# Per-head sums of squares on ScalarE, quarter-array raw products, one ring of PSUM banks and a new order, in a linear-attention plus gated-linear-unit kernel

## The chip, the cores and the metric

The kernel runs on one core of one Trainium2 chip. The metric is the device time of one execution in microseconds (us); a figure for a kernel is the median of its runs. The engines are TensorE (PE in the profile, with its weight loads as PEld), VectorE (DVE), ScalarE (ACT), GpSimd (POOL) and SyncE (SP, which here only issues DMAs). Each engine works through its own instructions in the order of the program, and waits on semaphores where it needs another's result.

## What is computed

The reference has two parts. The first is attention without a softmax, for 8 batches and 8 heads of 576 tokens and 64 columns; the second is a gated linear unit whose gate is a causal convolution over five tokens:

```python
kv = np.einsum('bhsd,bhse->bhde', k, v)
out = np.einsum('bhsd,bhde->bhse', q, kv)
rms = np.sqrt(np.mean(out * out, axis=-1, keepdims=True) + 1e-06)
x = out / rms * g_norm                    # then (B,H,S,D) -> (B, S, H*D): 8 x 576 x 512
xp = np.concatenate([np.zeros((B, K - 1, D)), x], axis=1)
for k in range(5):
    gate_pre += conv_w[k][None, None, :] * xp[:, k:k + S, :]
gate = 1.0 / (1.0 + np.exp(-gate_pre))
result = gate * (x @ w_val) @ w_out
```

q, k, v and the result are float32; the two weight matrices, 512 x 512, and conv_w arrive as float64 and are narrowed on the chip.

## The kernel before

All work is cut into small steps, and the text `PLAN` lists 1151 of them by name and arguments. The kernel runs through that list once and issues each step's instructions, so the list is the order of the work on every engine and in every DMA queue: two steps on one engine run in the listed order, and steps on different engines run as soon as what they wait for is there. There is no scheduler at run time.

A batch b has 576 tokens, in five chunks: 0 to 3 of 128 tokens and chunk 4 of 64. The steps of a batch, with the engine that does the work:

- `load_half`, `load_q`, `load_q_rows`, `stage_weight`: DMAs in, nearly all on SP's queue, with a few of the first on ACT's and POOL's queues. `narrow_weight w j n`, n from 0 to 7: the eight operations that turn a quarter of a float64 matrix into float32; n = 1, 2, 3 are ACT's, the others DVE's.
- `turn_q_rows` and `sort_q` (batches 0 and 1, PE and ACT) or `turn_q` (batches 2 to 7, DVE) put q with its columns on the partitions.
- `kv_product b i` (PE): k^T v of half of the heads, 36 products of 64 x 64 on the four quarters of the array, written at the front of `raws`. Between the two halves of batch 0 stand two filler products (`keep_warm 2`). `kv_copy b` (ACT, two instructions) moves the results into `kv_bd`, where two heads make one 128 x 128 block with zeros off the diagonal.
- The raw product q (k^T v): for batches 0 and 1 `raw_product b c` multiplies each chunk by the block-diagonal 128 x 128 matrices; for batches 2 to 7 `raw_pair b c` does two chunks at once as 64 products of 64 x 64 on quarters, and `raw_product b 4` does the last chunk with the blocks.
- `square b c` (ACT, one instruction for the whole chunk) writes the squares to SBUF, beside a 65th column that holds the epsilon; `sums b c` (DVE) adds each head's 65 columns up; `powers b c` (POOL) raises the sums to the power -1/2; `normalise b c` multiplies the raw product by that root, on DVE for batch 0 and on ACT for batches 1 to 7, where each head is one instruction. Two chunks of batch 0 take their roots from Newton steps on DVE (`roots`).
- x gets its columns onto the partitions through PE and ACT (`turn_x`, `keep_x`) or through DVE and small SBUF-to-SBUF DMAs issued by POOL (`turn_blocks`, `move_blocks`). `halo` (POOL) copies the convolution's overlap.
- The gate: `gate_start` (ACT), four `gate_tap` (DVE), `gate_end` (ACT, the sigmoid), `gated` (DVE, times the values).
- The values x w_val: `val_product` with `keep_val` for batches 0 and 1; for batches 2 to 7 a scheme with seven instead of eight block products (`x_sums`, `val_fast`, `val_keep`). The last product with w_out in pairs of batches: `out_product` with `keep_out`, or seven block products again (`token_sums`, `fast_product`, `fast_keep`); `store` sends the rows out.

PSUM has eight banks. Two of them are `raws`, kept for k^T v and most raw products; the other six are handed out by `ps(kind, ...)`: one of kind "tp" and five of kind "mm". Near the end `raws` is closed and its two banks serve the last products (`ends`). `warm_up`, near the head of the list, runs one Sigmoid on a single column.

Of the kernel before, what the change touches and what calls it, by code (L numbers as in the profile page):

```python
# [15 lines left out]
P = 128  # L16
# [3 lines left out]
load_q_rows 0 1; stage_weight cw 0; load_q_rows 0 0; load_half v 0 0; load_half k 0 0; load_half v 0 1;  # L20
load_half k 0 1; warm_up; stage_weight wval 1; stage_weight wval 0; start_warm 36; turn_q_rows 0 0;
turn_q_rows 0 1; narrow_weight cw 0 0; turn_q_rows 0 2; narrow_weight cw 0 1; narrow_weight cw 0 2; sort_q 0 0;
turn_q_rows 0 3; sort_q 0 1; turn_q_rows 0 4; narrow_weight cw 0 3; kv_product 0 0; sort_q 0 2;
load_q_rows 1 0; narrow_weight cw 0 4; narrow_weight cw 0 5; load_half k 1 0; sort_q 0 3; narrow_weight cw 0 6;
load_half v 1 0; narrow_weight cw 0 7; sort_q 0 4; load_q_rows 1 1; load_half k 1 1; stage_weight wval 2;
keep_warm 2; kv_product 0 1; stage_weight wval 3; turn_cw; load_half v 1 1; kv_copy 0; keep_cw;
narrow_weight wval 1 0; raw_product 0 3; load_half v 2 0; raw_product 0 2; square 0 3; raw_product 0 4;
sums 0 3; stage_weight wout 0; square 0 2; raw_product 0 1; square 0 4; powers 0 3; sums 0 2;
narrow_weight wval 1 1; sums 0 4; raw_product 0 0; load_half v 2 1; square 0 1; narrow_weight wval 0 0;
narrow_weight wval 0 1; powers 0 2; square 0 0; normalise 0 3; sums 0 1; turn_x 0 3; sums 0 0; keep_x 0 3;  # L30
powers 0 4; normalise 0 2; narrow_weight wval 1 2; narrow_weight wval 1 3; turn_x 0 2; normalise 0 4;
turn_q_rows 1 0; roots 0; keep_x 0 2; narrow_weight wval 0 2; turn_x 0 4; sort_q 1 0; turn_q_rows 1 1;
keep_x 0 4; narrow_weight wval 0 3; normalise 0 1; turn_q_rows 1 2; halo 0; sort_q 1 1; normalise 0 0;
turn_x 0 1; narrow_weight wval 1 4; kv_product 1 0; narrow_weight wval 0 4; keep_x 0 1; sort_q 1 2;
narrow_weight wval 0 5; turn_x 0 0; narrow_weight wval 1 5; narrow_weight wval 0 6; turn_q_rows 1 3;
keep_x 0 0; narrow_weight wval 0 7; gate_start 0 0; turn_q_rows 1 4; narrow_weight wval 1 6; kv_product 1 1;
sort_q 1 3; load_q 2 0; narrow_weight wval 1 7; gate_start 0 1; narrow_weight wval 2 0; val_product 0 0 1;
gate_start 0 2; narrow_weight wval 3 0; sort_q 1 4; load_q 2 1; gate_tap 0 2 3; kv_copy 1; gate_tap 0 0 3;
narrow_weight wval 3 1; raw_product 1 3; narrow_weight wval 2 1; gate_tap 0 1 3; load_half k 2 0;
raw_product 1 2; keep_val 0 0 1; gate_tap 0 0 2; square 1 3; narrow_weight wval 3 2; val_product 0 1 1;  # L40
sums 1 3; square 1 2; gate_tap 0 1 2; powers 1 3; narrow_weight wval 2 2; load_half k 2 1; gate_tap 0 2 2;
narrow_weight wval 2 3; stage_weight wout 2; raw_product 1 1; sums 1 2; narrow_weight wval 3 3;
narrow_weight wval 2 4; raw_product 1 0; keep_val 0 1 1; powers 1 2; square 1 1; narrow_weight wval 2 5;
normalise 1 3; val_product 0 0 0; load_q 2 2; gate_tap 0 0 1; sums 1 1; turn_q 2 0; normalise 1 2; powers 1 1;
turn_x 1 3; narrow_weight wval 3 4; val_product 0 1 0; narrow_weight wval 2 6; keep_x 1 3; load_q 2 3;
narrow_weight wval 3 5; square 1 0; narrow_weight wval 2 7; normalise 1 1; turn_x 1 2; sums 1 0;
raw_product 1 4; gate_tap 0 2 1; stage_weight wout 1; powers 1 0; kv_product 2 0; narrow_weight wout 0 0;
square 1 4; sums 1 4; narrow_weight wout 0 1; narrow_weight wval 3 6; kv_product 2 1; keep_x 1 2; turn_q 2 1;
powers 1 4; normalise 1 0; gate_tap 0 2 0; turn_x 1 1; load_q 3 0; val_product 0 2 1; narrow_weight wval 3 7;
keep_x 1 1; gate_tap 0 1 1; keep_val 0 1 0; narrow_weight wout 0 2; gate_tap 0 1 0; keep_val 0 0 0; turn_x 1 0;  # L50
normalise 1 4; gate_tap 0 0 0; val_product 0 2 0; narrow_weight wout 2 0; narrow_weight wout 0 3; keep_x 1 0;
narrow_weight wout 0 4; kv_copy 2; val_product 0 3 1; turn_q 2 2; keep_val 0 2 1; keep_val 0 2 0; turn_q 2 3;
narrow_weight wout 2 1; load_q 3 1; gate_end 0 0; narrow_weight wout 0 5; turn_x 1 4; narrow_weight wout 0 6;
raw_pair 2 3; keep_val 0 3 1; keep_x 1 4; gated 0 0; narrow_weight wout 2 2; stage_weight wout 3; halo 1;
val_product 1 0 1; narrow_weight wout 0 7; load_q 3 2; square 2 3; square 2 2; sums 2 3;
narrow_weight wout 2 3; sums 2 2; powers 2 3; gate_end 0 1; val_product 1 0 0; narrow_weight wout 1 0;
gate_end 0 2; narrow_weight wout 2 4; gate_start 0 3; gated 0 1; keep_val 1 0 1; narrow_weight wout 2 5;
powers 2 2; load_half v 3 1; val_product 1 1 1; normalise 2 3; gate_tap 0 3 3; load_half k 3 0;
load_half v 3 0; turn_q 3 0; narrow_weight wout 2 6; val_product 0 3 0; normalise 2 2; gated 0 2;
narrow_weight wout 2 7; turn_blocks 2 3; narrow_weight wout 1 1; load_q 3 3; raw_pair 2 1; gate_tap 0 3 2;  # L60
narrow_weight wout 1 2; narrow_weight wout 3 0; raw_product 2 4; keep_val 1 0 0; turn_q 3 1; square 2 1;
val_product 1 1 0; load_half k 3 1; keep_val 0 3 0; sums 2 1; narrow_weight wout 3 1; gate_tap 0 3 1;
square 2 0; powers 2 1; square 2 4; sums 2 0; narrow_weight wout 3 2; val_product 1 2 1; gate_tap 0 3 0;
keep_val 1 1 1; narrow_weight wout 1 3; turn_blocks 2 2; powers 2 0; narrow_weight wout 3 3;
narrow_weight wout 1 4; val_product 1 2 0; normalise 2 1; turn_q 3 2; narrow_weight wout 3 4; load_q 4 1;
normalise 2 0; narrow_weight wout 3 5; val_product 1 3 1; narrow_weight wout 3 6; sums 2 4; load_q 4 0;
keep_val 1 1 0; narrow_weight wout 3 7; powers 2 4; gate_end 0 3; turn_blocks 2 1; kv_product 3 0;
gate_start 1 0; narrow_weight wout 1 5; keep_val 1 2 1; gated 0 3; normalise 2 4; val_product 1 3 0;
narrow_weight wout 1 6; gate_start 1 1; gate_tap 1 0 3; narrow_weight wout 1 7; turn_x 2 4; kv_product 3 1;
turn_blocks 2 0; keep_x 2 4; gate_start 1 2; gate_tap 1 0 2; move_blocks 2 3; keep_val 1 3 0; out_product 0 1;  # L70
turn_q 3 3; load_half k 4 1; kv_copy 3; load_half k 4 0; gate_tap 1 2 3; keep_val 1 3 1; keep_val 1 2 0;
gate_tap 1 1 3; gate_tap 1 0 1; gate_tap 1 1 2; raw_pair 3 3; gate_tap 1 0 0; gate_tap 1 1 1; out_product 0 0;
square 3 3; move_blocks 2 2; gate_tap 1 2 2; keep_out 0 1; gate_end 1 0; store 0 1; sums 3 3; square 3 2;
gate_tap 1 2 1; gated 1 0; powers 3 3; load_q 4 2; sums 3 2; out_product 0 3; keep_out 0 0; gate_tap 1 1 0;
gate_start 1 3; gate_tap 1 2 0; powers 3 2; gate_end 1 1; gate_tap 1 3 3; normalise 3 3; gate_tap 1 3 2;
move_blocks 2 1; store 0 0; out_product 0 2; gate_tap 1 3 1; gate_end 1 2; normalise 3 2; gated 1 1;
gate_tap 1 3 0; load_half v 4 0; halo 2; gated 1 2; gate_end 1 3; val_sums 0; raw_pair 3 1; keep_out 0 2;
gated 1 3; keep_out 0 3; turn_blocks 3 3; store 0 2; raw_product 3 4; square 3 1; val_sums 1; out_product 0 5;
square 3 0; move_blocks 2 0; turn_q 4 0; load_half v 4 1; sums 3 1; turn_blocks 3 2; val_sums 2; powers 3 1;
load_q 4 3; sums 3 0; out_product 0 7; turn_q 4 1; keep_out 0 5; square 3 4; powers 3 0; turn_q 4 2;  # L80
load_q 5 0; normalise 3 1; weight_sums 0; sums 3 4; val_sums 3; powers 3 4; normalise 3 0; out_product 0 4;
turn_blocks 3 1; x_sums 2 0; x_sums 2 1; gate_start 2 2; normalise 3 4; gate_tap 2 2 3; gate_start 2 0;
turn_blocks 3 0; kv_product 4 0; turn_q 4 3; gate_tap 2 2 2; kv_product 4 1; x_sums 2 3; turn_x 3 4;
x_sums 2 2; kv_copy 4; load_half k 5 1; val_fast 2 0 0; store 0 5; gate_tap 2 2 1; keep_x 3 4; raw_pair 4 3;
move_blocks 3 3; val_keep 2 0 0; val_fast 2 0 1; store 0 3; square 4 3; square 4 2; sums 4 3; val_fast 2 0 2;
gate_start 2 1; sums 4 2; powers 4 3; val_fast 2 0 3; load_half k 5 0; gate_tap 2 1 3; val_keep 2 0 2;
# [773 lines left out]
```

## Time and profile before

| what | value |
| --- | --- |
| time, median of 3 runs | 314.0 us (313.92 to 314.35) |
| the profiled execution: span from first to last instruction | 313.7 us, so 0.3 us below the median time |
| PE busy | 302.8 us, 97% of the span, 3197 instructions |
| DVE busy | 255.7 us, 82% |
| ACT busy | 191.1 us, 61% |
| POOL busy | 133.4 us, 43% |
| granted TensorE clock | 1.000 |
| DMA | 55.50 MB, mean 177 GB/s |
| all `square` instructions (ACT) | 40 instructions, 21.6 us busy |
| the `sums` of 38 chunks (DVE) | 23.3 us busy |
| the `powers` of 38 chunks (POOL) | 65.4 us busy |
| all `normalise` instructions on ACT | 252 instructions, 55.3 us busy |

"Busy" is the time in which at least one instruction of the group runs; "mean ns of one" is the length of a single one, and neighbours on an engine overlap a little, so that the spacing of a dense run is shorter than the length of one. An instruction's line is that of the step's function. Each fp32 product shows as two records on PE, so 36 products of `kv_product` are 72 records.

### The profile page before, as it was taken

How to read it: one execution, taken by the hardware profiler on the slowest of the kernel's cores; microseconds unless marked ns; L12 is line 12 of the kernel's file. 1: busy time of each engine (PE TensorE's matmuls, PEld its weight loads, DVE VectorE, ACT ScalarE, POOL GpSimd, SP SyncE). 2: the span in 40 equal slices, each digit the busy share in tenths (PEclk: the TensorE clock that was granted, in tenths of full speed). 3: DMA queues.
4: the chain of work that ended last, by engine and by line, in shares of the span. 5: the costliest groups of instructions: out<-in, count | busy, mean ns of one | idle time of the engine just before them, and what ended most of it. 6: DMA issues, size and time to landing. Idle time of an engine off the chain costs nothing.

```text
span 313.7 us, 8362 instructions
## 1 busy us (share of the span) xinstructions
PE 302.8 (97%) x3197; PEld 217.6 (69%) x3197; DVE 255.7 (82%) x462; ACT 191.1 (61%) x542; POOL 133.4 (43%) x175
## 2 busy tenths in 40 slices
PE   7978999999999999999999999999999999999993
PEld 7866878777645485757666776587668868888582
DVE  1149899999999969899999899899998999764412
ACT  1457899999485867747685858485773343352120
POOL 3033073435588456666684659265749000000000
PEclk9999999999999999999999999999999999999999
DMA  7999597599677769668966986422335213022322
GB/s 276 377 386 352 149 294 219 173 298 239 186 189 210 210 188 342 196 168 276 270 155 194 251 251 160 118 50 54 100 78 127 58 25 88 0 67 57 89 73 85
DMA packets 26696, 55.50 MB, mean 177 GB/s; under 512 B 6166, under 2 KB 8214, under 8 KB 26656
## 3 DMA queue, kind: packets, MB, share of 16 engines
q1 hardware_dynamic: 22608, 46.61, 49.8%
q0 software_dynamic: 3168, 6.32, 7.9%
q10 hardware_dynamic: 880, 2.03, 1.9%
q8 instruction: 25, 0.41, 0.5%
q14 instruction: 15, 0.12, 0.1%
HBM read 39.21 MB, written 9.44 MB: 155 GB/s over the span
## 4 chain that ended last, share of the span: by engine, by line
PE 85%; ACT 5%; DMA 4%; DVE 2%; SPq 1%; issue 1%; POOL 1%; ACTq 0%; DVEq 0%
PE out L718 18%; PE va L687 15%; PE a L784 8%; PE vc L687 8%; PE cb L784 6%; PE val L637 6%; PE raw L438 5%; PE out L725 5%; PE raw L510 4%; PE vb L687 4%; PE qTps L472 3%; PE raw L493 2%; DMA k<-in_k_dram 2%; DMA qs<-in_q_dram 2%; PE xTps L587 1%; ACT x L572 1%
## 5 line engine op out<-in xcount | busy, mean ns | idle before, releaser
L625 DVE SCALAR_TENSOR_TENSOR gate<-xT,cwT,gate 128x576 f32<-128x576 f32 x128 | 101.0, 810 | 2.1 <-ACT gate L619 1.6
L546 POOL TENSOR_TENSOR rt<-ss,mhalf 128x8 f32<-128x8 f32 (+1 forms) x38 | 65.4, 1728 | 80.7 <-DVE ss L540 77.1
L608 POOL DMA_DIRECT2D xT<-y x96 | 52.8, 556 | 17.4 <-DVE xs L671 6.0
L718 PE MATMUL out<-wout,gv 128*128 128x512 f32 x128 | 57.3, 595 | 0.0
L572 ACT ACTIVATE x<-raw,rt 128x64 f32<-128x64 f32 x252 | 55.3, 369 | 2.2 <-POOL rt L546 1.6
L718 PEld LDWEIGHTS out<-wout,gv 128*128 128x128 f32 x128 | 23.9, 190 | 26.0 <-issue 24.1
L637 PE MATMUL val<-xT,wval 128*128 128x288 f32 x128 | 32.9, 409 | 0.1
L540 DVE TENSOR_REDUCE ss<-sq 128x8 f32<-128x520 f32 (+1 forms) x38 | 23.3, 626 | 8.3 <-ACT sq L528 8.1
L528 ACT ACTIVATE sq<-raw 128x512 f32<-128x512 f32 (+1 forms) x40 | 21.6, 564 | 12.4 <-PE raw L510 8.8
L637 PEld LDWEIGHTS val<-xT,wval 128*128 128x128 f32 x128 | 23.6, 190 | 6.3 <-ACT xT L594 0.3
L619 ACT ACTIVATE gate<-xT,cwT 128x576 f32<-128x576 f32 x32 | 25.2, 796 | 4.0 <-DVE gv L650 3.9
L687 PE MATMUL va<-xs,vsum 128*128 128x288 f32 x96 | 27.2, 406 | 0.0
L650 DVE TENSOR_TENSOR gv<-gv,gate 128x576 f32<-128x576 f32 x32 | 24.2, 762 | 3.0 <-ACT gate L632 2.8
L632 ACT ACTIVATE gate<-gate 128x576 f32<-128x576 f32 x32 | 22.1, 702 | 5.5 <-DVE gate L625 5.4
L687 PEld LDWEIGHTS va<-xs,vsum 128*128 128x128 f32 x96 | 18.2, 190 | 4.7
L733 ACT COPY ot<-out 128x512 f32<-128x512 f32 x20 | 12.0, 603 | 14.0 <-PE out L725 6.0
L438 PEld LDWEIGHTS raw<-v,k 64*64 64x64 f32 x1008 | 15.5, 135 | 4.7 <-issue 3.8
L793 DVE TENSOR_TENSOR ot<-cb,ot 128x256 f32<-128x256 f32 x16 | 6.7, 420 | 14.7 <-ACT ot L797 7.0
L615 POOL COPY xT<-xT 128x124 f32<-128x124 f32 x32 | 13.4, 456 | 10.3 <-ACT xT L594 10.3
L708 ACT COPY gv<-va 128x288 f32<-128x288 f32 x12 | 4.8, 400 | 19.8 <-PE va L687 19.8
L438 PE MATMUL raw<-v,k 64*64 64x64 f32 x1008 | 16.8, 220 | 0.0
L600 DVE STREAM_TRANSPOSE y<-x 128x512 f32<-128x512 f32 x24 | 16.7, 698 | 0.0
(119 smaller groups left out, 516.7 us busy)
## 6 DMA issues: line engine op xcount, KB each, us to landing
qs<-in_q_dram SPq DMA_DIRECT2D x96, 140.0 KB, 4.3
out_dram<-ot SPq DMA_DIRECT2D x140, 64.0 KB, 2.3
k<-in_k_dram SPq DMA_DIRECT2D x14, 576.0 KB, 6.5
v<-in_v_dram SPq DMA_DIRECT2D x12, 576.0 KB, 6.3
xT<-y POOLq DMA_DIRECT2D x96, 64.0 KB, 3.4
y<-in_moe_w_val_dram SPq DMA_DIRECT2D x4, 512.0 KB, 12.0
w_wout<-in_moe_w_out_dram SPq DMA_DIRECT2D x4, 512.0 KB, 7.2
qs<-in_q_dram SPq DMA_DIRECT2D x3, 576.0 KB, 5.4
```

The source lines that it names most:

```text
L438: nc.tensor.matmul(raws[r * D:(r + 1) * D, s, i * D:(i + 1) * D], st["k", b, i][rows, r, cols], st["v", b, i][rows, r, cols], start=(j == ...
L540: nc.vector.reduce_sum(out=ss[:, 0:n], in_=st["sq", b, c][:, 0:n], axis=AX.X)
L546: nc.gpsimd.tensor_tensor(out=rt[:, 0:n], in0=st["ss", b, c][:, 0:n], in1=mhalf[:, 0:n], op=ALU.pow)
L572: nc.scalar.activation(out=x[:, to * D:(to + 1) * D], in_=one, func=AF.Copy, scale=st["rt", b, c][:, h:h + 1])
L608: nc.gpsimd.dma_start(out=xTs[b % 2][i * TB:(i + 1) * TB, :, first:first + P], in_=y[a * TB:(a + 1) * TB, i])
L619: nc.scalar.activation(out=gate[:], in_=xTs[b % 2][:, jt, HALO:SX], func=AF.Copy, scale=cwT[:, K - 1, jt:jt + 1])
L625: nc.vector.scalar_tensor_tensor(out=gate[:], in0=xTs[b % 2][:, jt, tap * TB:tap * TB + S], scalar=cwT[:, tap, jt:jt + 1], in1=gate[:], op ...
L637: nc.tensor.matmul(val[:], wval[:, kc, jt * P:(jt + 1) * P], xTs[b % 2][:, kc, HALO + n * SV:HALO + (n + 1) * SV], start=(kc == 0), stop=( ...
L650: nc.vector.tensor_tensor(out=both, in0=both, in1=st["gate", b, jt][:], op=ALU.mult)
L687: nc.tensor.matmul(st[bank, "val", b, mj][:], weights_[:, k], tokens()[:, k], start=(n in (0, 1, 3) and k == 0), stop=(k == NK // 2 - 1), ...
L718: nc.tensor.matmul(po[:], gv[:, jt, first:first + P], wout[:, jt, :], start=(jt == 0), stop=(jt == NK - 1),)
L784: nc.tensor.matmul(st[bank, i, p], tokens()[:, k], weights_[:, k], start=(n < 2 and k == 0), stop=(k == NK // 2 - 1), skip_group_check=True)
```

## The change

Four things change, and the order is written anew.

1. `square b c` becomes one ACT instruction for each head, on 128 x 64, which also writes the head's sum with `accum_out`; the step `sums` goes. The epsilon is added by a small DVE instruction, `add_eps`. `powers` takes the roots of a range of columns, for batch 0 of two chunks at once (`ROOTS`); the Newton step `roots` goes.
2. All raw products are made of 64 x 64 products on quarters, for all batches and the last chunk as well (`raw_pair`, `raw_tail`), in two banks each. `kv_bd` with its zeros becomes `kvs`; `kv_product` writes two banks of its own, and `kv_copy b s` copies one of them. `normalise` on DVE becomes two instructions for a chunk.
3. PSUM becomes one pool of eight banks, given out one by one.
4. `keep_warm` is dropped.

`PLAN` again has 1151 steps: 40 `sums`, one `roots`, one `keep_warm` and 16 `raw_product` are gone, and there are 38 `add_eps`, 8 `raw_tail`, 4 more `raw_pair` and 8 more `kv_copy`. All others keep their number and move. `warm_up` moves from the head of the list to the middle of batch 3. The diff, cut to its core:

```diff
 PLAN = """
-load_q_rows 0 1; stage_weight cw 0; load_q_rows 0 0; load_half v 0 0; load_half k 0 0; load_half v 0 1;
-load_half k 0 1; warm_up; stage_weight wval 1; stage_weight wval 0; start_warm 36; turn_q_rows 0 0;
...
+load_q_rows 0 1; start_warm 36; load_q_rows 0 0; load_half k 0 0; load_half v 0 1; load_half v 0 0;
+turn_q_rows 0 2; turn_q_rows 0 0; turn_q_rows 0 1; turn_q_rows 0 3; stage_weight cw 0; load_half k 0 1;
+stage_weight wval 0; stage_weight wval 1; kv_product 0 0; narrow_weight cw 0 0; sort_q 0 0;
+narrow_weight cw 0 1; narrow_weight cw 0 2; narrow_weight cw 0 3; sort_q 0 1; sort_q 0 3; kv_product 0 1;
+sort_q 0 2; kv_copy 0 0; kv_copy 0 1; load_half v 1 0; turn_q_rows 0 4; narrow_weight wval 0 0;
+narrow_weight wval 0 1; raw_pair 0 3; narrow_weight wval 0 2; sort_q 0 4; narrow_weight wval 0 5; raw_pair 0 1;
+load_q_rows 1 1; load_q_rows 1 0; square 0 3; add_eps 0 3; raw_tail 0; powers 0 3; square 0 2; square 0 4;
...
+add_eps 3 0; turn_blocks 3 2; normalise 3 1; turn_blocks 3 1; val_sums 2; val_fast 2 1 0; val_fast 2 0 0;
+val_keep 2 0 0; load_half k 5 1; val_fast 2 1 1; store 0 3; powers 3 0; val_keep 2 1 1; val_fast 2 0 1;
+val_fast 2 1 3; val_fast 2 0 2; load_half k 5 0; normalise 3 0; val_keep 2 1 0; gate_start 2 0; raw_tail 3;
...
-    BANKS = {"tp": 1, "mm": 5}
-
-    early = ExitStack()
-    raws = early.enter_context(tc.tile_pool(name="raws", bufs=1, space=bass.MemoryType.PSUM)).tile(
-        [P, 2, C], FP32, tag="raw", bufs=1, name="raw")
-
-    def ps(kind, shape, name):
-        return psum.tile(shape, FP32, tag=kind, bufs=BANKS[kind], name=name)
-
-    kv_bd = [const.tile([P, HP, P], FP32, name=f"kvbd{i}") for i in range(2)]
+
+    def ps(shape, name):
+        return psum.tile(shape, FP32, tag="bank", bufs=8, name=name)
+
+    kvs = [const.tile([P, HP, D], FP32, name=f"kv{i}") for i in range(2)]
...
+    ROOTS = {(0, 2): H + H // 2, (0, 1): 2 * H}
...
     def kv_product(b, i):
 
+        if ("kvps", b) not in st:
+            st["kvps", b] = [ps([P, 2, D], f"kvps{b}_{s}") for s in range(2)]
         for j in range(NR):
             for r in range(2):
                 for s in range(2):
                     rows, cols = slice(s * D, (s + 1) * D), slice(j * D, (j + 1) * D)
                     nc.tensor.matmul(
-                        raws[r * D:(r + 1) * D, s, i * D:(i + 1) * D],
+                        st["kvps", b][s][r * D:(r + 1) * D, i],
                         st["k", b, i][rows, r, cols], st["v", b, i][rows, r, cols],
                         start=(j == 0), stop=(j == NR - 1))
 
-    def kv_copy(b):
-        for r in range(2):
-            rows = slice(r * D, (r + 1) * D)
-            nc.scalar.copy(
-                out=kv_bd[b % 2][rows, :, rows].rearrange("p (i s) e -> p s i e", s=2),
-                in_=raws[rows, :, 0:2 * D].rearrange("p s (i e) -> p s i e", i=2))
+    def kv_copy(b, s):
+        nc.scalar.copy(out=kvs[b % 2][:].rearrange("p (i s) e -> p s i e", s=2)[:, s], in_=st["kvps", b][s][:])
...
+    def raw_product(b, *chunks):
+        banks = [ps([P, len(chunks), C // 2 if chunks[0] < NJ else P], f"raw{b}_{chunks[0]}_{r}") for r in range(2)]
+        for n, c in enumerate(chunks):
+            st["raw", b, c] = [bank[:, n] for bank in banks]
         for hp in range(HP):
...
+            for c in chunks:
+                for half in range(2) if c < NJ else (hp // 2,):
+                    first = c * P + (half * D if c < NJ else 0)
                     for r in range(2):
                         rows, cols = slice(r * D, (r + 1) * D), slice(half * D, (half + 1) * D)
+                        to = hp if c < NJ else hp % 2
                         nc.tensor.matmul(
+                            st["raw", b, c][r][cols, to * D:(to + 1) * D],
+                            st["qT", b][rows, hp, first:first + D], kvs[b % 2][rows, hp, :],
+                            start=True, stop=True)
+
+    def raw_pair(b, c):
+        raw_product(b, c, c - 1)
+
+    def raw_tail(b):
+        raw_product(b, NJ)
...
     def square(b, c):
...
-        nc.scalar.activation(
-            out=sq[:, 0:n, 0:D] if n < H or b < PAIRS else sq[:, :, 0:D].rearrange("p (r h) e -> p r h e", r=2),
-            in_=by_head(b, c), func=AF.Square,
-        )
-
-    def sums(b, c):
...
-        nc.vector.reduce_sum(out=ss[:, 0:n], in_=st["sq", b, c][:, 0:n], axis=AX.X)
-        st["ss", b, c] = ss
+        for h in range(n):
+            to = FIRST[c] + h
+            nc.scalar.activation(
+                out=squared[:], in_=st["raw", b, c][h // (n // 2)][:, h % (n // 2) * D:(h % (n // 2) + 1) * D],
+                func=AF.Square, accum_out=st["ss", b][:, to:to + 1])
+
+    def add_eps(b, c):
+        ss = st["ss", b][:, root_range(b, c)]
+        nc.vector.tensor_scalar(out=ss, in0=ss, scalar1=D * EPS, scalar2=None, op0=ALU.add)
 
     def powers(b, c):
...
+        which = root_range(b, c)
         nc.gpsimd.tensor_tensor(
+            out=st["rt", b][:, which], in0=st["ss", b][:, which], in1=mhalf[:, which], op=ALU.pow)
```

## The prediction, made before any run of the changed kernel

> **What bounds the kernel now.** I read the totals first, then busy times by stage, then the chain that ended last, then the groups that the change touches. The totals:
>
> ```profile
> PE 302.8 (97%) x3197; PEld 217.6 (69%) x3197; DVE 255.7 (82%) x462; ACT 191.1 (61%) x542; POOL 133.4 (43%) x175
> ```
>
> TensorE is near full, DVE second. The stages (stretch, its length, then PE, PEld, DVE, ACT and POOL busy) show where that holds:
>
> ```profile
> 16.00:46.00 30.00, 26.41 (x395) 22.25 (x387) 23.72 (x52) 23.43 (x54) 10.97 (x10) 1.00 0.87 297
> 46.00:80.00 34.00, 33.80 (x478) 26.51 (x476) 33.23 (x62) 33.06 (x103) 13.74 (x12) 1.00 0.79 224
> 80.00:116.00 36.00, 36.00 (x491) 20.10 (x489) 33.16 (x54) 23.00 (x68) 23.40 (x30) 1.00 0.74 207
> 116.00:256.00 140.00, 140.00 (x1373) 97.04 (x1373) 130.81 (x220) 91.22 (x274) 82.87 (x116) 1.00 0.58 161
> ```
>
> From 59 us on PE never waits, so relief of DVE is worth nothing there. From 46 to 80 us ACT is as full as PE: 33.06 of 34.00. The chain (start, length, what) runs through ACT before 59 us and through PE after it:
>
> ```profile
> 13.68 1.91 PE warm L429 x4
> ...
> 47.49 1.63 ACT x L572 x8
> ...
> 53.06 0.62 ACT wexp_wout L364
> ...
> 53.97 0.83 ACT x L572 x4
> ...
> 58.99 8.03 PE val L637 x32
> ...
> 112.49 1.09 PE raw L510 x64
> 113.58 1.17 PE vc L687 x4
> 114.75 0.97 PE va L687 x4
> ```
>
> It gives spacings of dense runs: 0.204 us for a head's normalisation (1.63 / 8), 0.62 for a narrowing step, 0.97 for four records of a value product. The quarter products cost an entry and an exit: the product after them takes 1.17 instead of 0.97, and 64 records take 1.09 where 72 of k^T v take 1.21, so 8 take 0.12, 64 would be 0.96, and about 0.13 to 0.23 is entry. I take 0.2 for each boundary. The groups (busy, mean ns of one):
>
> ```profile
> L572 ACT ACTIVATE x<-raw,rt 128x64 f32<-128x64 f32 x252 | 55.3, 369 | 2.2 <-POOL rt L546 1.6 <-DVE y L600 0.3
> L540 DVE TENSOR_REDUCE ss<-sq 128x8 f32<-128x520 f32 x30 | 20.2, 684 | 8.2 <-ACT sq L528 8.1
> L528 ACT ACTIVATE sq<-raw 128x512 f32<-128x512 f32 x32 | 18.4, 601 | 12.0 <-PE raw L510 8.8 <-PE raw L493 3.1
> L546 POOL TENSOR_TENSOR rt<-ss,mhalf 128x8 f32<-128x8 f32 x30 | 55.7, 1865 | 71.2 <-DVE ss L540 71.0
> L546 POOL TENSOR_TENSOR rt<-ss,mhalf 128x4 f32<-128x4 f32 x8 | 9.7, 1214 | 9.5 <-DVE ss L540 6.1 <-ACT gate L619 3.4
> ```
>
> **PE, part by part.** The filler goes: -1.9. The raw products of batches 0 and 1 stream the same columns as blocks or quarters (four times 128 columns against 32 times 64, four at a time): 0. The last chunk has 8 small products for 4 wide ones: 0.6 us became 0.4 to 0.5 by the spacing of 64 records, -0.1 each, -1 in all. I counted in both lists where PE changes shape: boundaries that touch quarters go from 46 to 56 (five of the eight tails now stand alone among full products), +2.0; other boundaries between full and half-wide products from 21 to 12, at the 0.15 by which 16 half-wide records exceed 8 full ones (3.58 against 3.43), -1.3. Sum about -2. PE's own work by these spacings is 292 us before and 290 after.
>
> **The filler and the clock.** In the stretches 22 to 24 and 24 to 26 us PE was busy 0.67 and 0.77 of 2 us, yet the granted clock stayed 1.00, so I charge nothing for gaps where filler was. [...]
>
> **ACT.** 40 squares (21.6 us) become 288 instructions of 128 x 64 from PSUM. No row shows an accumulating one. Above: two instructions like L572 for each head, 0.43. Below: copies of 128x512 and 128x256 take 0.603 and 0.385, so 64 columns 0.22, less the 0.15 by which L572's length exceeds its spacing: 0.07, the accumulator free. I take 0.22, because L572 (55.3 / 252 = 0.219) is nearest: same shape, same source, one per-partition operand more than a plain copy. So 288 x 0.22 = 63 us, ACT +42. The 16 copies of k^T v stay about as they are. `warm_up` leaves the head, so ACT's first function is now a copy or a shift of exponents and the first Sigmoid comes later: a second table load is possible, 0 to 1.3 us (the one load in the trace lasts 1283 ns). I take 1.3, as it would fall into a full stretch of ACT.
>
> **DVE, POOL, SP.** DVE loses 24.6 of sums, 1.6 of Newton steps and 1.0 of memsets, and gains 38 `add_eps` of 0.16 (a 128x1 multiply takes 154 to 159 ns) = 6, and 0.5 for split normalisations: -20, worth nothing after 59 us where PE covers it. If DVE's cover fails, it was busy 33.23 of 34.00 in the full stretch, so the relief stops DVE from being what is late next. POOL's power grows by 0.16 us a column (1.865 - 1.214 over 4): 2.5 for 12 and 3.1 for 16 columns, one power more in batch 0, in a queue 43% full; between two `move_blocks` (four issues of 0.56) a power can wait 2.2 us, and ACT's normalisation behind it on ACT's queue waits as long: inside the idle term below. SP's loads and stores keep their number; DMA share is 0.9 up to 46 us, where a late k or q of batch 1 would cost 1 to 2 us, and I set it against the filler's gain there.
>
> **The sum.** ACT works in the listed order, so I added up its list as far as `normalise 3 0`, which frees the banks that `raw_tail 3` takes among eight full ones. Ahead of and with it stand 140 head squares (30.8), 104 head normalisations at 0.207 (21.5), 24 narrowing steps (14.8), 16 copies of values (4.6), 17 gate steps (10.6), 11 `keep_x` (4.8), 10 `sort_q` and 3 small narrowings (5.0), 10 `kv_copy` (2.1), 5 `keep_out` and 2 `val_keep` (2.9): 97.1 us. In the old list the same point has 74.4. The first square began at 19.75 us; without filler (1.9), with the last transposes of q behind k^T v (0.6) and two chunks in 1.09 instead of 2.07 (1.0) it begins near 16.2, 3.7 of the list being done. So the list ends at 16.2 + 93.4 + 1.3 = 110.9 without a gap. In 46 to 80 us ACT idled 3%, in 16 to 46 us 22%; I take 5%, nearer to the dense stretch, 5 us: 116. From `raw_tail 3` on PE has 195.1 us: 78 value products (75.7), 56 (48.4) and 14 (48.0) output products, raw products (8.4), k^T v (5.8), turns (1.4) and 7.4 of boundaries; that makes 311.1. After the last product of the old kernel's final stretch the work listed and the end differ by 5.6 (292.3 to 313.7 with 15.8 of products); a wait of 0.9 us at 300 us for banks goes with the ring: 4.6. That gives 315.7, so a span near 316, and a time 0.3 above it at most: 316. By the same way of adding, the old kernel is PE's 292 + 6.2 for the first q + 1.7 of slow first transposes + 8 of gaps before 59 us + 5.6 = 313.5. PE falls by 2 and its gaps before 115 us grow by about 5.
>
> **Rivals.** *PE stays the bound, and the time falls.* PE alone would reach `raw_tail 3` at 6.2 + 1.7 + 5.5 + 94.4 = 108 (5.5 of gaps); ACT's list ends before that if a head's square costs under 0.17 us (110.9 + 5 - 140 x 0.055 = 108). Then 290 + 6.2 + 1.7 + 3 to 8 of gaps + 4.6 = 305.5 to 310.5, 308. For it: an instruction without a pointer should be shorter than L572; against it: the accumulator has to be written out. *The accumulator costs a second instruction.* At 0.31 the list grows by 140 x 0.09 = 12.6: 328. At 0.43 ACT lags through batch 7: 194 + 284 x 0.21 to `raw_tail 7`, started 12.5 later, with 8 idle and 1.3 of table load, 275, and 77 of PE and 4.6 of end behind it: 357. *The ring stalls PE after batch 3*: values now hold up to six banks at once, and if each of the batches 3 to 7 makes PE wait 1 to 2 us for a bank, 5 to 10 us: 321 to 326.
>
> [...]
>
> **How the numbers follow.** What a measurement can tell from no change is about 0.2%, 0.6 us. ACT bound near 0.22 (0.19 to 0.26, idle 2.6 to 9 us: 309 to 326): chance 0.50, of which 0.16 faster, 0.07 same, 0.27 slower. PE bound: 0.25, 0.24 of it faster. Second instruction: 0.20. Ring: 0.05. Together faster 0.40, same 0.08, slower 0.52. The range 306 to 329 leaves out most of the dear accumulator and the edge below.
>
> **What would show it.** Right: ACT over 95% busy from 16 to 115 us with PE waiting on ACT there, PE full after it, squares 0.20 to 0.25 apart, DVE near 235 us busy, ACT near 233. Wrong: PE full from 46 us on with ACT idle (PE rival); squares 0.3 apart and ACT full up to 220 us (accumulator); PE waits on bank readers after 120 us (ring); a granted clock under 1.00 in the head (filler).

## The result and the profile after

The changed kernel takes 344.1 us in the median (341.7 to 345.4) against 314.0 beside it: a ratio of 1.0932, 95% interval 1.0881 to 1.0984. It is slower, as forecast, but by 30 us where 2 were forecast, and far outside the range. Of the runs below, one execution each of e2 and e12 and two of e10 ran slower than the kernel's others at a lower clock; figures are medians of the other runs. The page of the kernel after, totals and granted clock over 40 slices:

```profile
PE 308.6 (90%) x3449; PEld 217.6 (63%) x3449; DVE 237.0 (69%) x450; ACT 252.9 (74%) x1079; POOL 135.7 (40%) x175
...
PEclk9887999997899999999999999999999999999999
```

TensorE (PE) has 6 us more of busy time and 35 us without work in its span of 343.6 (11 before). The granted clock of TensorE, 1.00 throughout before, is below that in parts of the first third. The stages of the kernel after (stretch, length, then PE, PEld, DVE, ACT and POOL busy, clock, DMA share, GB/s):

```profile
16.00:46.00 30.00, 22.51 (x549) 19.52 (x542) 13.37 (x37) 26.35 (x128) 8.49 (x4) 0.88 0.69 219
46.00:80.00 34.00, 30.09 (x474) 23.13 (x473) 26.34 (x50) 33.30 (x118) 10.02 (x12) 1.00 0.94 265
80.00:116.00 36.00, 32.62 (x456) 20.54 (x455) 26.79 (x46) 33.03 (x154) 17.48 (x22) 0.91 0.57 146
116.00:256.00 140.00, 130.28 (x1404) 82.96 (x1397) 104.39 (x194) 120.83 (x575) 81.53 (x103) 1.00 0.63 167
```

Up to 116 us ACT is nearly full (33.3 of 34, 33.0 of 36) and PE is not; before, PE was full there from 46 us on. After 116 us, where PE had been busy 140.00 of 140, it now misses 9.7. The groups of the kernel after (busy, mean ns of one, idle before):

```profile
L499 ACT ACTIVATE squared<-raw 128x64 f32<-128x64 f32 x288 | 65.7, 228 | 13.7 <-PE raw L476 5.5
...
L499 ACT ACTIVATION_READ_ACCUMULATOR squared<-raw 128x1 f32 x288 | 57.4, 199 | 0.0
```

One line of the code has become two instructions on ACT: the square, and a read of the accumulator. ACT's timeline (start, length) gives their rhythm:

```profile
19.12 0.23 ACT L499 ACTIVATE squared<-raw 128x64 f32<-128x64 f32 x1
19.24 0.20 ACT L499 ACTIVATION_READ_ACCUMULATOR squared<-raw 128x1 f32 x1
19.47 0.22 ACT L499 ACTIVATE squared<-raw 128x64 f32<-128x64 f32 x1
19.59 0.19 ACT L499 ACTIVATION_READ_ACCUMULATOR squared<-raw 128x1 f32 x1
19.82 0.22 ACT L499 ACTIVATE squared<-raw 128x64 f32<-128x64 f32 x1
```

A head costs 0.35 us (19.47 to 19.82); over the dense run from 19.12 to 22.94, eleven heads, 0.347. I had taken 0.22. The chain that ended last names a second trouble, in the head:

```profile
1.68 11.73 DMA v<-in_v_dram
...
13.55 3.63 PE kvps L422 x144
...
33.96 0.19 SPq L302
...
36.53 10.30 DMA v<-in_v_dram
```

k^T v waits for v's first half, now queued behind the second, and the 144 records take 3.63 us where 72 took 1.21 before (the clock was 0.50 from 14 to 16 us). Later the loads stand in SP's queue behind one that waited 10.8 us for PE, by the profile for `turn_cw`; its issue ends at 34 us, and a load of v behind it lands at 47 us. From SP's waits (total, times, longest):

```profile
SPq L302 <- PE cwps L396: 10.8, 1, 10.8
```

### The profile page after: what moved, and what is told of

Same layout as the page of the kernel before. It is cut to its first block, busy times and chain, and to the rows that moved or that the text cites. A ratio compares the mean times of both kernels' runs of the same rounds, so it can differ in the third digit from the quotient of the medians.

```text
span 343.6 us, 9409 instructions
## 1 busy us (share of the span) xinstructions
PE 308.6 (90%) x3449; PEld 217.6 (63%) x3449; DVE 237.0 (69%) x450; ACT 252.9 (74%) x1079; POOL 135.7 (40%) x175
## 4 chain that ended last, share of the span: by engine, by line
PE 44%; DMA 21%; ACT 17%; DVE 6%; issue 4%; SPq 3%; POOL 3%; ACTq 0%; DVEq 0%; POOLq 0%
DMA v<-in_v_dram 10%; ACT squared L499 9%; DMA qs<-in_q_dram 8%; PE va L635 8%; PE a L726 7%; PE out L666 6%; PE cb L726 6%; ACT x L524 4%; PE kvps L422 4%; PE vc L635 3%; PE out L673 3%; PE val L586 3%; POOL xT L557 2%; SPq L302 2%; PE raw L476 2%
## 5 line engine op out<-in xcount | busy, mean ns | idle before, releaser
L512 POOL TENSOR_TENSOR rt<-ss,mhalf 128x8 f32<-128x8 f32 (+3 forms) x38 | 66.4, 1748 | 118.1 <-DVE ss L508 112.2
L499 ACT ACTIVATE squared<-raw 128x64 f32<-128x64 f32 x288 | 65.7, 228 | 13.7 <-PE raw L476 5.5
L524 ACT ACTIVATE x<-raw,rt 128x64 f32<-128x64 f32 x252 | 56.3, 383 | 3.0 <-POOL rt L512 3.0
L499 ACT ACTIVATION_READ_ACCUMULATOR squared<-raw 128x1 f32 x288 | 57.4, 199 | 0.0
L586 PE MATMUL val<-xT,wval 128*128 128x288 f32 x128 | 35.2, 433 | 0.2 <-ACT kv L428 0.2
L508 DVE TENSOR_SCALAR ss<-ss 128x8 f32<-128x8 f32 (+3 forms) x38 | 6.3, 166 | 39.0 <-ACT squared L499 38.9
L422 PE MATMUL kvps<-v,k 64*64 64x64 f32 x1008 | 20.6, 233 | 11.2 <-DMA v<-in_v_dram 5.7
L422 PEld LDWEIGHTS kvps<-v,k 64*64 64x64 f32 x1008 | 18.6, 147 | 16.4 <-issue 9.2
L476 PEld LDWEIGHTS raw<-kv,qT 64*64 64x64 f32 x1152 | 20.1, 134 | 11.7 <-issue 3.5
L476 PE MATMUL raw<-kv,qT 64*64 64x64 f32 x1152 | 23.5, 222 | 3.6 <-issue 2.1
L438 DVE STREAM_TRANSPOSE qT<-qs 128x512 f32<-128x512 f32 x24 | 16.8, 700 | 3.4 <-DMA qs<-in_q_dram 3.4
## 6 DMA issues: line engine op xcount, KB each, us to landing
y<-in_moe_w_val_dram SPq DMA_DIRECT2D x4, 512.0 KB, 10.8
```

Source lines behind the costliest of these rows:

```text
L422: nc.tensor.matmul(st["kvps", b][s][r * D:(r + 1) * D, i], st["k", b, i][rows, r, cols], st["v", b, i][rows, r, cols], start=(j == 0), sto ...
L476: nc.tensor.matmul(st["raw", b, c][r][cols, to * D:(to + 1) * D], st["qT", b][rows, hp, first:first + D], kvs[b % 2][rows, hp, :], start=T ...
L499: nc.scalar.activation(out=squared[:], in_=st["raw", b, c][h // (n // 2)][:, h % (n // 2) * D:(h % (n // 2) + 1) * D], func=AF.Square, acc ...
L512: nc.gpsimd.tensor_tensor(out=st["rt", b][:, which], in0=st["ss", b][:, which], in1=mhalf[:, which], op=ALU.pow)
L524: nc.scalar.activation(out=x[:, to * D:(to + 1) * D], in_=raw[:, h * D:(h + 1) * D], func=AF.Copy, scale=root[:, to:to + 1])
L586: nc.tensor.matmul(val[:], wval[:, kc, jt * P:(jt + 1) * P], xTs[b % 2][:, kc, HALO + n * SV:HALO + (n + 1) * SV], start=(kc == 0), stop=( ...
```

## The experiments

I held two theories at first. A: the accumulator's second instruction makes ACT's list late, and that is nearly all. B: the new order, its loads, the ring and long runs of small products make PE late whatever ACT does. Later runs split B: H and Q (instructions of the quarter products arrive late), F (the filler held the clock), R (the ring), L (loads in the head), S (spread over the list). P and V ask where on the list the accumulator costs.

### e1_chunk_new: the change without part 1

```diff
-        for h in range(n):
-            to = FIRST[c] + h
-            nc.scalar.activation(out=squared[:], in_=..., func=AF.Square, accum_out=st["ss", b][:, to:to + 1])
+        for r, raw in enumerate(st["raw", b, c]):        # one instruction for a bank
+            nc.scalar.activation(out=sq[:, r * n // 2:(r + 1) * n // 2, 0:D], in_=..., func=AF.Square)
 def add_eps(b, c):
+            nc.vector.reduce_sum(out=st["ss", b][...], in_=st["sq", b, one][:, 0:n], axis=AX.X)
```

> The changed kernel with its new order, ring and quarters, but squares by whole banks (two ScalarE instructions for a chunk) and sums by a VectorE reduction where the small addition stood. Theory A (ScalarE is the bound because a head's square takes 0.347 us there, an ACTIVATE and a read of the accumulator): ScalarE's work falls by 288 x 0.347 - 80 x 0.27 = 78 us, it is no longer the bound, and the time falls to 309 to 320. Theory B (the new order costs: loads that stand late on SyncE's queue, waits for PSUM banks, TensorE waiting in runs of small products): 330 to 344, with TensorE still idle some 30 us.

Measured 333.3 us (1.058, 1.0528 to 1.0632). So the accumulator accounts for 10.8 of the 30 us in the new order, and 19 remain without it: B. Where `raw_tail 3`, the point on which the forecast's sum turns, begins on PE:

```profile
121.55 0.47 PE L479 MATMUL raw<-kv,qT 64*64 64x64 f32 x16
```

and in the kernel after:

```profile
131.25 0.32 PE L476 MATMUL raw<-kv,qT 64*64 64x64 f32 x2
132.03 0.47 PE L476 MATMUL raw<-kv,qT 64*64 64x64 f32 x14 [0.46 <-ACT x L524]
```

The kernel after passes it at 132.0, held by ACT's normalisation (L524); without the accumulator it passes at 121.6, held by no one at that point. The two points lie 10.5 us apart, of the 12.3 us by which these two executions differ (343.6 and 331.3 us of span); from there both need 210 to 212 us.

### e2_no_read: head squares without the accumulator

```diff
-            nc.scalar.activation(out=squared[:], ..., func=AF.Square, accum_out=st["ss", b][:, to:to + 1])
+            nc.scalar.activation(out=squared[:, i, h], ..., func=AF.Square)
```

The sums are left out: the roots are taken from other numbers.

> The changed kernel with the same 288 squares of single heads but without the accumulator output; the roots are then taken of other numbers (columns of the squares) and the result is not the reference's. Theory A: no read instruction, squares some 0.10 to 0.13 apart, ScalarE's work less by 288 x 0.22 = 63 us, time 310 to 322, near the run with squares by banks. Theory B: 330 to 344.

Measured 331.0 us, in one run, about what e1 took (330.6 to 334.0). ACT's timeline of this run:

```profile
20.12 2.44 ACT L500 ACTIVATE squared<-raw 128x64 f32<-128x64 f32 x20 [0.26 <-PE raw L477]
```

Twenty squares in 2.44 us with 0.22 for the last one: 0.117 apart. So it is neither the number of squares nor their length that costs, but the read: with it they are 0.347 apart.

### e3_accum_old: part 1 alone, in the old kernel

```diff
-        nc.scalar.activation(out=sq[...], in_=by_head(b, c), func=AF.Square)      # one a chunk
+        for h in range(n):
+            nc.scalar.activation(out=sqs[:], in_=one, func=AF.Square, accum_out=ss[:, h:h + 1])
 def sums(b, c):
-        nc.vector.reduce_sum(out=ss[:, 0:n], in_=st["sq", b, c][:, 0:n], axis=AX.X)
+        nc.vector.tensor_scalar(out=ss, in0=ss, scalar1=D * EPS, scalar2=None, op0=ALU.add)
```

> The kernel before (its order, its raws and filler) with only the squares changed: one ScalarE instruction for each head with the accumulator, and a small addition on VectorE in place of the sum. Theory A: ScalarE's list grows by 288 x 0.347 - 18 = 82 us; at the first half of batch 4 it stands 142 us long where TensorE's is 114, so 15 + 28 minus the 8 it started behind: the time rises by 20 to 35, to 334 to 349. Theory B: the accumulator is hidden behind TensorE and the time stays at 314 to 322.

Measured 386.1 us (1.2274, 1.2209 to 1.2339). Both theories were far too low. In the old order the accumulator costs 71 us: a chunk's eight heads take 2.8 us on ACT (8 x 0.347), everything listed behind them waits, and PE waits for ACT's copies of values (13.4 us in one row of its waits, 9.2 in another) and for x. With the new order, ring and quarters 10.8 us of that are left: what the same instructions cost depends on what the list puts behind them.

### e4_chunk_old: ring and quarters in the old order

The old list with the new steps (`raw_pair`, `raw_tail`, split `kv_copy`), no filler, squares by banks as in e1.

> The old order with the rest of the change but the accumulator: quarters for all raw products, ring of eight banks, no filler, squares by banks and sums on VectorE. Theory A: ring, quarters and filler are worth next to nothing: 311 to 316. Theory B in the form that the ring or the runs of small products cost: 320 to 330; in the form that only the order costs: 311 to 316 here, and 330 or more in the run with squares by banks in the new order.

Measured 320.75 us (1.0204, 1.0168 to 1.024). So the new order alone is worth +12.6 us (e1 against e4), and ring, quarters, squares by banks and the missing filler together +6. PE's timeline in the head of e4 shows how:

```profile
15.44 1.15 PE L475 MATMUL raw<-kv,qT 64*64 64x64 f32 x60 [0.17 <-ACT kv L427]
19.83 2.62 PE L475 MATMUL raw<-kv,qT 64*64 64x64 f32 x84 [3.24 <-issue]
```

Within one step, with all operands there, PE stood still for 3.24 us for nothing that the profile names ("issue"). The stretches behind it (the third number from the end is the clock, the next the DMA share):

```profile
18.00:22.00 4.00, 2.17 (x81) 2.17 (x82) 1.07 (x2) 1.49 (x6) 0.29 (x1) 0.73 1.03 402
22.00:26.00 4.00, 1.71 (x20) 1.11 (x13) 3.54 (x10) 3.43 (x9) 3.96 (x3) 0.50 1.07 394
26.00:30.00 4.00, 4.00 (x28) 3.01 (x30) 3.55 (x18) 3.24 (x7) 0.06 (x1) 0.50 0.97 377
```

Half the clock until 30 us, where PE turns q and x: the four records of a turned chunk take 1.09 us there and 0.66 from 31.6 us on.

### e5_no_filler and e6_fill_back: the filler by itself

e5 is the kernel before without `keep_warm 2`; e6 is e4 with two filler products of 128 x 512 between the halves of batch 0's k^T v.

> The kernel before with nothing changed but that the filler products between the halves of batch 0's k^T v are left out. Theory H (a long unbroken run of quarter products outruns TensorE's instructions; a hole of 2 to 3 us follows, and the granted clock halves after it): here the run is 144 records of k^T v and then full-width raw products, shorter than the 204 records ahead of the hole in e4_chunk_old, so no hole over 1 us and 313 to 315 us. Theory F (the filler itself held the clock): granted clock under 0.9 in the stretch from 16 to 30 us, and 317 to 322 us. Theory R (ring and quarters alone make the 6 us of e4_chunk_old): 312.5 to 315 us, clock 1.00.

> e4_chunk_old with the filler put back between the halves of batch 0's k^T v (two products of 128 x 512). Theory H: the filler gives the instructions 1.9 us to catch up, so the hole of 3.2 us at 16.6 us goes or shrinks under 1 us, the clock stays 1.00 from 16 to 30 us, and 314 to 317 us. Theory F: also 314 to 317 us, but e5_no_filler is slow as well. Theory R (ring, quarters and split squares cost it all along the list): 319 to 321.5 us.

Measured 315.6 us (1.0024, 1.0000 to 1.0047) and 320.85 us (1.0208, 1.0161 to 1.0255). In time the filler is worth nothing that can be told either way, so F's price is out, although its sign came: the clock in e5 was 0.68 from 22 to 26 us. H is out in its first form (a run that is too long), since in e6 the filler gave 1.9 us of rest and the hole, of 2.33 us, still came after the 56th record of the raw product:

```profile
17.02 1.04 PE L484 MATMUL raw<-kv,qT 64*64 64x64 f32 x56 [0.20 <-ACT kv L436]
20.39 2.65 PE L484 MATMUL raw<-kv,qT 64*64 64x64 f32 x88 [2.33 <-issue]
```

Counted from the start of the program the hole stands at one and the same place in e4 and e6: in e4 72 records of `start_warm`, 72 of turned q, 144 of k^T v, 1 of `turn_cw`, 60 of the raw product, in e6 four of filler more and four of the raw product less, 349 in both. The time of e6 is what R forecast; e9 below tries R itself.

### e7_head_loads_banks and e8_head_loads_accum: the loads in the head

```diff
-load_q_rows 0 1; start_warm 36; load_q_rows 0 0; load_half k 0 0; load_half v 0 1; load_half v 0 0;
+load_q_rows 0 1; start_warm 36; load_q_rows 0 0; load_half k 0 0; load_half v 0 0; load_half v 0 1;
...
-stage_weight wval 0; stage_weight wval 1; kv_product 0 0; narrow_weight cw 0 0; sort_q 0 0;
+stage_weight wval 0; stage_weight wval 1; turn_q_rows 0 4; load_q_rows 1 1; load_q_rows 1 0; kv_product 0 0;
```

and `narrow_weight cw 0 4` to `7`, `turn_cw` and `keep_cw` moved up beside the first k^T v; e7 on e1, e8 on the kernel after.

> e1_chunk_new (new order, ring and quarters, squares by banks) with four things moved in the head of its list: v's first half loaded ahead of its second, the last transposes of batch 0's q ahead of k^T v, with them the loads of batch 1's q, and the convolution weights narrowed and turned at once. Theory L (the new order's loss of 12.6 us against e4_chunk_old is the head's loads, which stand behind those steps in SP's queue): the wait for batch 1's q at 24.7 us and SP's waits of 9.3 and 6.8 us go, and 322 to 327 us. Theory S (the loss is spread over the list: banks, gaps from instruction issue in runs of quarters, order of the gates): 330 to 334 us.

> The kernel after with the same four moves in its head as e7_head_loads_banks. Theory L with ACT hidden behind it: 333 to 338 us. Theory A (ACT's list of accumulating squares, 0.346 us for a head, is what is late, so that earlier loads only make TensorE wait for ACT instead): 341 to 345 us. Theory S: 341 to 345 us, with the gaps of TensorE before instruction issue and banks as before.

Measured 330.0 us (1.0476, 1.0412 to 1.0540) and 343.5 us (1.0929, 1.0873 to 1.0985). The 330.0 us lie at the edge of S's range and outside L's: earlier loads are worth 3.4 us without the accumulator, by the medians (the intervals just touch), and nothing that can be measured with it. PE's waits of e8 (total, times, longest) say why:

```profile
PE qTps L446 <- ACT squared L493: 5.3, 1, 5.3
PE raw L470 <- issue: 4.8, 2, 3.5
```

PE's waits for q fell from 4.1 us in the kernel after to 0.4 and those for v from 5.7 to 4.0, but the waits for ACT's squares rose from 2.2 to 5.3. The hole before "issue" now shows as well (3.5 us, in e7 too, at the 349th record again); in the kernel after, PE had waited 3.5 us for v shortly ahead of that record, and ran through it without a hole (144 records in 2.46 us from 17.62 us). Waits taken away uncovered others behind them.

### e9_blocks_old_order and e10_blocks_new_order: no quarters in the head

```diff
 def raw_product(b, *chunks):
+        if b < 2:
+            for c in chunks:
+                raw_blocks(b, c)          # four products with the 128 x 128 blocks of kv_bd, one bank
+            return
```

with `kv_bd` and its zeros back for batches 0 and 1; e9 on e4, e10 on e7.

> e4_chunk_old with the raw products of batches 0 and 1 made by block-diagonal 128 x 128 products again (40 records for a batch instead of 144); the ring, the old order, no filler, the squares by banks stay. Theory Q (quarters in the head: TensorE's instructions arrive in packets some 6 us apart while the DMA engines are full, and 144 records at 0.017 us use them up; the hole at the 348th record costs 3.2 us, and half the clock after it): no hole over 1 us before 60 us, granted clock 1.00 or a short dip, 314 to 317 us. Theory R (the ring of banks, such as k^T v of batch 2 waiting 2.55 us for a bank at 52 us, makes the 6 us): 318.5 to 321 us.

> e7_head_loads_banks with the same blocks for batches 0 and 1. Theory Q: the hole of 3.5 us at 16.6 us, the half clock behind it and the hole at 34.4 us go, and 320 to 325 us. Theory S (the rest of the new order's loss is spread along the list, in waits for loads and gates after 60 us): 327 to 331 us.

Measured 311.4 us (0.9906, 0.9874 to 0.9939), below Q's range, and 322.0 us (1.0235, 1.0184 to 1.0285). Q's sign and size are borne out, while its reading that instructions arrive late is not shown by these times: 104 records less for each of two batches go with 9.4 us less in the old order and, by the ratios, 7.6 less in the new one. The hole of 3.2 us and the half clock behind it are part of that. The blocks also take one bank a chunk where the quarters take two for a pair, and e4's wait of 2.55 us for a bank at 52 us goes too; no run parts that from the records. PE's timeline of e9, and its stretch of 18 to 22 us:

```profile
12.53 2.41 PE L424 MATMUL kvps<-v,k 64*64 64x64 f32 x144
14.87 0.23 PE L398 MATMUL cwps<-ident,cw 21*128 21x21 f32 x1
15.57 4.96 PE L480 MATMUL raw<-kvbd,qT 128*128 128x128 f32 x40 [0.47 <-ACT kvbd L433]
```

```profile
18.00:22.00 4.00, 3.31 (x28) 2.57 (x28) 3.56 (x8) 3.91 (x11) 3.42 (x3) 1.00 1.03 405
```

PE has no hole before "issue" here, and the clock stays at 1.00. e9 is also faster than the kernel before, by 0.6 to 1.3%: the first raw product starts at 15.57 us instead of 17.66, and the run of value products that began at 58.99 us before begins at 55.32; that lead of 3.7 us is kept to the end (span 309.7 for 313.7). It differs from e5, which gained nothing, by the ring, the squares and sums by banks and, in batches 2 to 7, quarters for the last chunk. Which of these brings it was not tried. R is out as the ring by itself: with the ring in place PE's waits in e9 add up to no more than before (5.4 us and 5.6), and the 2.55 us for a bank at 52 us don't appear.

### e11_fewer_warm_records: where the hole stands

`start_warm 36` of 32 columns became `start_warm 10` of 128 columns in e4: 52 records less at the front.

> e4_chunk_old with 10 first warming products of 128 columns instead of 36 of 32 columns, so 52 records less ahead of the same work. Theory Q (the hole stands at a fixed count of instructions from the start): the hole moves from the 60th record of the first raw pair to about the 112th of the 144, starts about 0.9 us later and is shorter by as much; 319 to 321 us. A rival (the hole belongs to the place, the second half of the first raw pair, for instance to a bank or to the writes there): it stays at the 60th record with 3.2 us.

Measured 319.6 us (1.0159, 1.0107 to 1.0211). PE's timeline:

```profile
12.38 1.11 PE L421 MATMUL kvps<-v,k 64*64 64x64 f32 x58 [0.90 <-DMA k<-in_k_dram]
15.64 0.46 PE L421 MATMUL kvps<-v,k 64*64 64x64 f32 x14 [2.15 <-issue]
...
16.44 3.32 PE L475 MATMUL raw<-kv,qT 64*64 64x64 f32 x112 [0.18 <-ACT kv L427]
22.04 0.69 PE L475 MATMUL raw<-kv,qT 64*64 64x64 f32 x32 [2.28 <-issue]
```

The hole moved by 52 records to the 112th, as Q has it: 20 + 72 + 144 + 1 + 112 is 349 again, and it shrank by 0.96 us. What I had not expected is a second one, of 2.15 us, 127 records ahead of it. The two together are longer than e4's one, and the time is not clear of e4's (1.0168 to 1.0240).

### e12_late_accum and e13_early_accum: where the accumulator costs

`if b <= 3` squares by banks with DVE's sums and otherwise heads with the accumulator; e13 the reverse.

> The kernel after, with squares by banks and DVE's sums for batches 0 to 3, and the accumulating head squares only for batches 4 to 7. Theory P (the prediction's frame: ACT's list as far as batch 3's last normalisation sets the end; 140 accumulating squares of 0.346 us stand in it, and later ones are covered by TensorE): 333 to 336 us, like e1_chunk_new. Theory V (the accumulating squares cost all along the list, as each chunk's sums come later): half of the 10.8 us between e1_chunk_new and the kernel after, 337 to 340 us.

> The reverse: accumulating head squares for batches 0 to 3 alone, squares by banks and DVE's sums for batches 4 to 7. Theory P: 341 to 344 us, as the kernel after. Theory V: 337 to 340 us.

Measured 334.0 us (1.0616, 1.0532 to 1.0699) and 341.4 us (1.0816, 1.0757 to 1.0874). Of the 11.1 us that the ratios of e1 and the kernel after make, the accumulators of batches 0 to 3 bring 7.4 (e13 against e1) to 10.0 (e12 against the kernel after), and the others 1.1 to 3.7. So it is mostly P; the intervals leave room for a part of V. In e13 `raw_tail 3` goes on at 130.9 us.

## Why the prediction was wrong, by its steps

*The direction held, and the frame in the main.* ACT's list as far as `normalise 3 0` does set when `raw_tail 3` runs (e1 and e13), though ACT was 93% busy from 16 to 116 us where over 95 was the sign, and PE lost time in the head to loads besides. The second table load came (1283 ns), DVE's busy time is 237 where about 235 was forecast, and its relief brought nothing: e2, without sums on DVE, takes about as long as e1 with them. With a forecast of +2 us and a chance of 0.52 for slower, the right direction is partly luck.

*The failing step is the price of a head's square*: 0.22 taken, 0.347 measured. By the forecast's own sum 140 x 0.127 makes 17.8 us, and with a first square at 19.1 instead of 16.2 the list would end at 116 + 17.8 + 2.9 = 136.7; it ended at 132.0 (ACT idle 6.7 us in between, for 5 forecast, the rest of the list some 6 us shorter than added up). So 16 of the 28 us that the forecast missed stand ahead of that point. The nearest row was the wrong one: L572 is one instruction, and the accumulated sum is delivered by another (199 ns in the mean). The rival had this, between prices of 0.31 and 0.43, and the range stopped short of it.

*The remainder of PE was the second term.* 199.7 us were worked out from `raw_tail 3` to the end, 211.6 passed: 199.1 busy for 195.1, 8.1 of waits up to 330 us for none, and an end of 4.4 for 4.6. In e1 it is 209.8 without any accumulator, so most of it belongs to the rest of the change. The waits are small and of several kinds: in the kernel after 1.7 and 1.0 us of value products for ACT's copies and 1.6 of k^T v for v, in e1 one of 4.5 of k^T v for DVE's turned q. The old kernel waited nowhere in this part up to 300 us, and I carried that over to a list that I had not gone through for loads and banks.

*"The raw products stream the same columns: 0"* was wrong twice. On the array the quarters are shorter, as the prediction itself had it where it set 1.09 us against 2.07 for two chunks; batch 0's raw product before and after, from PE's timelines:

```profile
17.66 4.63 PE L493 MATMUL raw<-kvbd,qT 128*128 128x128 f32 x40 [0.70 <-ACT kvbd L446]
```

```profile
17.62 2.46 PE L476 MATMUL raw<-kv,qT 64*64 64x64 f32 x144
```

And yet the time is 9.4 us longer with them in the old order (e4 against e9); the hole of 3.24 us before "issue" and the half clock behind it are part of that. The list gives the count (3449 records for 3197), and the prediction put no price on it. That also breaks the first rival: PE alone was to reach `raw_tail 3` at 108 us and to end at 308; in e1, with ACT's list short, it is 121.6 and 331 (span), of which PE is busy 303. What holds e1 is PE with its waits, 23 us later than I put it.

*The filler at nothing* was right in time (e5), though not for the reason given: the clock did fall without it, to 0.68 from 22 to 26 us, and by e5's time what ran slower there cost the end next to nothing. *The ring* cost nothing by itself (e9). *SP's loads* at 1 to 2 us were 3.4 without the accumulator (e7).

Together, by the ratios to the kernel before: ring, tails and no filler -0.9% (e9), quarters in batches 0 and 1 to +2.0% (e4), the new order to +5.8% (e1), the accumulator to +9.3%. The parts aren't independent: e10 shows the new order at +2.4% with better loads and blocks, still 10.6 us over e9. Of these PE's busy time makes 3.6 and its gaps 7.0; the waits of e10 are many and short, the longest of them:

```profile
PE kvps L422 <- DVE ss L536: 2.6, 1, 2.6
PE kvps L422 <- DMA k<-in_k_dram: 2.3, 1, 2.3
PE kvps L422 <- DMA v<-in_v_dram: 1.7, 2, 1.4
PE kvps L422 <- issue: 1.6, 1, 1.6
```

The list is that of a kernel without sums on DVE, and e10 has them; no run takes it apart further, and it stays open.

## What to carry to other kernels

An output that an instruction also gives can be an instruction of its own on the engine's queue (here 199 ns beside a square of 228): until a trace shows one, put the dear price into the likeliest case, not into a rival. A finer tiling multiplies an engine's instructions, even where it shortens the work itself: batch 0's raw product took 2.46 us as 144 records and 4.63 as 40, and yet the kernel took 9.4 us longer with quarters in batches 0 and 1 (e4 against e9). In such a head, count instructions as you count bytes. And where several engines are late at once, taking one wait away only shows the next: the parts of such a change must be tried in both orders before one is called the cause.

## What the runs showed of the hardware

The page of the kernel after has a DMA queue that the profile calls instruction (packets, MB, share of the 16 engines):

```profile
q8 instruction: 27, 0.44, 0.6%
```

The kernel before has 25 packets there. No view says whose instructions they are. As an estimate, if they were PE's and PEld's alone, 2 x 3449 of them in 27 packets would be 255 for a packet (2 x 3197 in 25 would be 256), which is 128 records of a product; the two holes in e11 stand 127 records apart. At the spacings measured, quarter products use up 128 records in 2.15 us (1.21 for 72), value products of 128 x 288 in some 31 (0.97 for four).

The holes at the 349th record in e4, e6, e8 and e11 last 3.24, 2.33, 3.51 and 2.28 us. That they are waits for a packet is my estimate from those distances, and was not shown.

Nor is it shown that full DMA engines delay the packets. By quarter-microsecond windows of the DMA view they moved at 9.75, 17 and 29.75 us in the kernel before, at a DMA share of 1.03 to 1.10 from 12 to 30 us, and at 10.25, 16, 22.25 and 30.5 us in the kernel after, where the share was 0.08 from 16 to 18 us and 1.0 from 20 to 26; no run emptied the engines.

A hole of 2.33 us in e6 (0.06 us of PE work from 18 to 20 us) was followed by a clock of 0.50 from 22 up to 30 us, although PE was busy 5.6 of those 8 us. In the kernel before, with the filler ahead of them, gaps of 1.33 and 1.23 us that end at 23.61 and 25.51 us left it at 1.00 (PE busy 1.44 of 4.00 us from 22 to 26 us); without the filler (e5) it was 0.68 there, with PE busy 2.76:

```profile
22.00:26.00 4.00, 2.76 (x18) 2.22 (x20) 3.62 (x13) 3.04 (x6) 1.77 (x2) 0.68 1.09 362
```

What brings the clock down is not shown by these runs.
